# Sixteen one-column copies leave GpSimd for VectorE or ScalarE in a fused attention and FFT-mixing kernel

## The chip, the cores and the metric

The kernel runs on one core of one Trainium2 chip. The metric is the device time of one execution in microseconds (us), as a median over several executions. A profile takes one execution; its "span" was 1.8 us shorter than that execution's device time, so profiles and times can be set against each other. A run over 1.5% above the fastest of its kernel would be set aside as slow.

## The reference, cut to what matters

```
attn = softmax(normalise(q) @ normalise(k).T / tau) @ v     # 8 batches, 12 heads, 448 tokens, 64 wide
x    = heads of attn side by side                            # (8, 448, 768)
u    = x + real(fft(fft(x, axis=1), axis=2))
out  = u + relu(layernorm(u) @ w_ch1) @ w_ch2                # 768 -> 3072 -> 768
```

The two FFTs are matrix products with cosine and sine tables. The kernel halves them by folding: it adds and subtracts mirrored rows (giving F) and mirrored columns (giving G). Columns 0 and 192 of the fold are their own mirror images, so they are not added to anything; they are copied. That is one copy of a 128x8 tile per such column, two per batch, 16 in all.

## The kernel before

The program has its own list scheduler: each operation is planned with an estimated length and put at the end of one engine's queue, and each engine then runs its queue strictly in that order, waiting on semaphores (in the trace of this kernel VectorE's 893 instructions, ScalarE's 677 and TensorE's 5625 weight loads start in the line order of the built program). An operation planned for two engines goes to whichever the plan finds free first.

```python
        if dj < 2:                                     # in fold(): the self-mirrored column of block dj
            c = 192 * dj
            P.add("pool", lambda g: g.tensor_copy(G[:, :, :, c:c + 1], F[:, :, :, c:c + 1]), 0.25, pj, f"gc{dj}_{b}",
                  reads=[f"F0{dj}", f"F1{dj}"], writes=[f"Gc{dj}"])
        # ... cut: VectorE makes the rest of G (L834)
        # row FFT of this block, 8 matmuls (L847); it waits for G and for the copy
        P.add("pe", fn, 8 * t_mm(NK), pj, f"fs{blk}_{b}", reads=[f"Gc{blk}", f"G{blk}0", f"G{blk}1", "CSs"], ...)
```

GpSimd also issues the weight loads, twelve pieces of W1 and twelve of W2, at most three in flight: each issue waits until the load three places earlier has landed.

```python
            # in weights(): prev[-3] is the load three places earlier
            prev.append(P.add("pool", fn, 0.8, 9, nm, writes=[nm], dma=(nm, 16), after=[prev[-3]], serve=2.1))
```

Up to the first FFN matmul, the program fills planned pauses of TensorE with small matmuls ("fillers", L1097) whose results nobody reads. They are there to keep the engine busy: in the first profile, where they stop at 45.77 us and the engine stands, its granted clock falls to 0.50 from 48.7 to 58.9 us.

```python
                for _ in range(n):
                    r = pe.matmul(self.PS[:, bank, 450:512], self.ID[:], self.ID[:, 0:62], start=True, stop=True)
```

Of the kernel before, what the change touches and what calls it, by code (L numbers as in the profile page):

```python
# [290 lines left out]
def t_act(n, ptr=0):  # L291
    return 0.12 + 0.00089 * n + 0.093 * ptr


def t_dve(n, mode=1):
    return 0.1 + n / (960.0 * mode)
# [6 lines left out]
def t_mm(n):  # L303
    return max(0.036, n / 2400.0 + 0.0025)


def gp(ap, dims, off=0):

    return bass.AP(ap.tensor, ap.offset + off, [list(ap.ap[0])] + [list(d) for d in dims])


class Kern:
# [491 lines left out]
    def fold(self, b, dj, pj):  # L804

        P = self.P
        X = self.X[:].rearrange("p a (s c) -> p a s c", s=2)[:, :, :, 128 * dj:128 * dj + 128]
        AC, F, G = self.AC, self.F, self.G
        xr = [f"X{dj}", f"X{dj + 3}"]
        for i, o in ((0, AluOp.add), (2, AluOp.subtract)):  # L810
            P.add("dve", lambda v, i=i, o=o: v.tensor_tensor(AC[:, i:i + 2], X[:, 0:2], X[:, 2:4], o),
                  t_dve(512, 2), pj, f"fa{dj}_{b}", reads=xr, writes=[f"AC{i}"])
        for eo, o in ((0, AluOp.add), (1, AluOp.subtract)):
            op = P.add("dve", lambda v, eo=eo, o=o: v.tensor_tensor(F[:, eo, :, 128 * dj:128 * dj + 128], AC[:, :, 0, :], AC[:, :, 1, :], o),
                       t_dve(512, 2), pj, f"f{eo}{dj}_{b}", reads=["AC0", "AC2"],
                       writes=[f"F{eo}{dj}"] + ([f"UN{x}" for x in range(4)] if dj == 0 and eo == 0 else []),
                       after=[self.first_f] if dj or eo else [])
            if dj == 0 and eo == 0:
                self.first_f = op
        if dj < 2:  # L820

            c = 192 * dj
            P.add("pool", lambda g: g.tensor_copy(G[:, :, :, c:c + 1], F[:, :, :, c:c + 1]), 0.25, pj, f"gc{dj}_{b}",
                  reads=[f"F0{dj}", f"F1{dj}"], writes=[f"Gc{dj}"])
        if dj == 0:
            return

        blk = 2 - dj if dj == 2 else 1
        c0, n, m = ((1, 127, 128), (128, 64, 65))[blk]
        for i, o in ((0, AluOp.add), (1, AluOp.subtract)):  # L830
            def fn(v, i=i, o=o):
                f0, fs_ = (0, 2304) if i == 0 else (768, 768)
                g0, gs = (0, 6 * NG) if i == 0 else (2 * NG, 2 * NG)
                return v.tensor_tensor(gp(G[:], [[gs, 2], [NG, 2], [1, n]], g0 + c0), gp(F[:], [[fs_, 2], [384, 2], [1, n]], f0 + c0),  # L834
                                       gp(F[:], [[fs_, 2], [384, 2], [-1, n]], f0 + 384 - c0), o)
            P.add("dve", fn, t_dve(4 * n), pj, f"g{blk}_{b}", reads=[f"F{x}{y}" for x in range(2) for y in ((0, 2), (1, 2))[blk]],
                  writes=[f"G{blk}{i}"])
        tile = Tile("G")

        def fn(pe):  # L840
            bk = self.bank(tile)
            for eo in range(2):
                for s in range(2):
                    o = self.PS[0:m, bk + eo, s * NK:(s + 1) * NK]
                    for t in range(2):
                        k = 128 if t == 0 else RB
                        r = pe.matmul(o, G[0:k, eo, 2 * s + t, blk * 128:blk * 128 + m],  # L847
                                      self.CSs[0:k, t, s, :], start=(t == 0), stop=(t == 1))
            return r
        P.add("pe", fn, 8 * t_mm(NK), pj, f"fs{blk}_{b}", reads=[f"Gc{blk}", f"G{blk}0", f"G{blk}1", "CSs"], tiles=(tile,), acquire=tile, margin=0.2)  # L850
        for es, ah in ([(("act",), (0,)), (("dve",), (1,))] if b == 0 and blk else [(("act", "dve"), (0, 1))]):
            def ev(e, ah=ah):
                bk, a = self.bank(tile), slice(ah[0], ah[-1] + 1)
                o = self.Tt[0:m, 0:4 * SQ2].rearrange("p (a d k) -> p d a k", a=2, d=2)[:, blk, a]
                i = self.PS[0:m, bk + ah[0]:bk + ah[-1] + 1, 0:SQ2]
                if e is self.nc.scalar:
                    return e.activation(o, i, ACTF.Copy)  # L857
                return e.tensor_copy(o, i)
            n_ = len(ah) * SQ2
            P.add(es, ev, [t_act(n_) if e == "act" else t_dve(n_) for e in es], pj, f"te{blk}_{b}",  # L860
                  writes=[f"Tt{blk}" + ("b" if len(ah) == 1 and ah[0] else "")], after=[tile.users[0]], tiles=(tile,))
# [294 lines left out]
```

## Time and profile before

| | value |
|---|---|
| time, median of 3 | 625.41 us (624.96 to 626.06) |
| the profiled execution | 627.76 us, span 625.9 us |
| TensorE busy | 594.1 us, 95% of the span |
| VectorE, ScalarE, GpSimd busy | 63%, 55%, 16% |
| mean granted TensorE clock of the profiled execution | 0.986 |

Read it from the engine that is nearly always busy, and look for what its pauses wait for. The prediction below shows the lines.

### The profile page before, as it was taken

How to read it: one execution, taken by the hardware profiler on the slowest of the kernel's cores; microseconds unless marked ns; L12 is line 12 of the kernel's file. 1: busy time of each engine (PE TensorE's matmuls, PEld its weight loads, DVE VectorE, ACT ScalarE, POOL GpSimd, SP SyncE). 2: the span in 40 equal slices, each digit the busy share in tenths (PEclk: the TensorE clock that was granted, in tenths of full speed). 3: DMA queues.
4: the chain of work that ended last, by engine and by line, in shares of the span. 5: the costliest groups of instructions: out<-in, count | busy, mean ns of one | idle time of the engine just before them, and what ended most of it. 6: DMA issues, size and time to landing. Idle time of an engine off the chain costs nothing.

```text
span 625.9 us, 13629 instructions
## 1 busy us (share of the span) xinstructions
PE 594.1 (95%) x5607; PEld 388.3 (62%) x5625; DVE 391.3 (63%) x893; ACT 342.7 (55%) x677; POOL 98.4 (16%) x141
## 2 busy tenths in 40 slices
PE   4784889999999999999999999999999999999998
PEld 4564767767777566665646666666556666654464
DVE  7972997698777868887796679678644460010011
ACT  7870689426885388658666846772765015104400
POOL 8722411201003100300300040003000010010010
PEclk9996899999999999999999999999999999999999
DMA  7999949939729924985956299429200130000001
GB/s 185 123 212 208 148 77 190 90 94 188 131 55 121 183 69 95 137 154 117 128 69 158 70 122 165 90 53 133 65 1 2 39 88 26 25 28 25 1 26 75
DMA packets 187630, 62.03 MB, mean 99 GB/s; under 512 B 166704, under 2 KB 185264, under 8 KB 187568
## 3 DMA queue, kind: packets, MB, share of 16 engines
q1 hardware_dynamic: 129648, 38.35, 33.0%
q0 software_dynamic: 57920, 22.81, 27.7%
q8 instruction: 44, 0.72, 0.5%
q14 instruction: 18, 0.15, 0.1%
HBM read 51.90 MB, written 11.01 MB: 101 GB/s over the span
## 4 chain that ended last, share of the span: by engine, by line
PE 85%; DMA 5%; POOL 4%; DVE 3%; ACT 2%; issue 1%; POOLq 0%; DVEq 0%
PE PS L1000 35%; PE PS L1022 33%; PE PS L751 5%; PE PS L782 5%; DMA W1b<-in_moe_w_ch_dram 5%; PE PS L847 2%; PE PS L779 2%; PE PS L882 2%; ACT E L733 1%; DVE U L903 1%; PE PS L763 1%; PE PS L764 1%; POOL VB L713 1%; POOL UNT L440 0%; DVE ST L930 0%
## 5 line engine op out<-in xcount | busy, mean ns | idle before, releaser
L1000 PE MATMUL PS<-UNT,W1b 128*128 128x256 bf16 (+3 forms) x1423 | 232.7, 317 | 2.9 <-issue 1.0
L1022 PE MATMUL PS<-W2b,hT 128*128 128x384 bf16 (+2 forms) x1343 | 228.9, 326 | 0.1
L1000 PEld LDWEIGHTS PS<-UNT,W1b 128*128 128x128 bf16 x1440 | 130.4, 99 | 86.5 <-issue 3.0
L1022 PEld LDWEIGHTS PS<-W2b,hT 128*128 128x128 bf16 x1344 | 129.2, 98 | 82.3 <-issue 2.0
L733 ACT ACTIVATE E<-PS 128x900 bf16<-128x900 f32 (+1 forms) x192 | 149.8, 826 | 32.1 <-PE PS L751 26.6
L1009 ACT ACTIVATE hT<-PS 128x512 bf16<-128x512 f32 (+3 forms) x166 | 79.6, 480 | 99.5 <-PE PS L1000 98.0
L1031 DVE TENSOR_TENSOR OUTB<-PS,U 128x384 f32<-128x384 f32 (+2 forms) x56 | 31.2, 557 | 117.6 <-PE PS L1022 116.8
L1052 POOL DMA_INDIRECT out_dram<-OUTB,IDX x20 | 21.4, 1071 | 252.7 <-DVE OUTB L1031 118.1
L668 DVE TENSOR_REDUCE SS<-QH 128x6 f32<-128x384 f32 x84 | 45.3, 540 | 11.5 <-ACT QH L666 11.3
L1010 DVE TENSOR_SCALAR hT<-PS 128x256 bf16<-128x256 f32 (+3 forms) x74 | 37.0, 501 | 23.1 <-PE PS L1000 21.8
L782 PE MATMUL PS<-VB,E 128*128 128x65 bf16 x1152 | 51.0, 193 | 0.0
L782 PEld LDWEIGHTS PS<-VB,E 128*128 128x128 bf16 x1152 | 47.7, 97 | 1.6
L666 ACT ACTIVATE QH<-STG 128x384 f32<-128x384 f32 x84 | 43.5, 518 | 6.4 <-DVE SS L668 3.3
L751 PE MATMUL PS<-QT,KT 64*128 64x225 bf16 x576 | 42.9, 261 | 2.1 <-ACT E L733 1.7
L779 PE MATMUL PS<-VZ,E 128*128 128x130 bf16 x192 | 42.2, 220 | 1.6 <-DMA VB<-in_v_dram 1.3
L903 DVE TENSOR_TENSOR U<-SQT,X 128x384 bf16<-128x384 f32 (+3 forms) x80 | 41.0, 552 | 0.8
L675 DVE TENSOR_TENSOR QH<-STG,RN 128x768 bf16<-128x768 f32 x42 | 39.8, 950 | 0.3
L857 ACT ACTIVATE Tt<-PS 128x900 bf16<-128x900 f32 (+2 forms) x14 | 12.5, 892 | 40.5 <-PE PS L847 40.5
L796 DVE TENSOR_TENSOR X<-PS,RD 128x512 bf16<-128x512 f32 x48 | 33.1, 691 | 1.5
L751 PEld LDWEIGHTS PS<-QT,KT 64*128 64x128 bf16 x576 | 21.2, 94 | 20.3 <-ACT E L733 7.5
L713 POOL DMA_DIRECT2D VB<-in_v_dram x24 | 25.3, 1061 | 41.9 <-PE PS L782 41.6
L934 ACT ACTIVATE RS<-MV,cst 128x1 f32<-128x1 f32 x28 | 8.2, 291 | 42.4 <-DVE MV L932 41.1
(116 smaller groups left out, 491.5 us busy)
## 6 DMA issues: line engine op xcount, KB each, us to landing
STG<-in_q_dram SPq DMA_DIRECT2D x18, 384.0 KB, 4.9
STG<-in_k_dram SPq DMA_DIRECT2D x18, 384.0 KB, 4.7
VB<-in_v_dram POOLq DMA_DIRECT2D x24, 192.0 KB, 5.9
W1b<-in_moe_w_ch_dram POOLq DMA_DIRECT2D x12, 384.0 KB, 8.8
W2b<-in_moe_w_ch_dram POOLq DMA_DIRECT2D x12, 384.0 KB, 6.9
out_dram<-OUTB SPq DMA_DIRECT2D x7, 384.0 KB, 2.9
hT<-in_k_dram SPq DMA_DIRECT2D x2, 576.0 KB, 5.4
hT<-in_q_dram SPq DMA_DIRECT2D x2, 576.0 KB, 6.8
```

Of the source, the lines that this page charges most:

```text
L666: P.add("act", lambda a, sq=sq, src=buf[:, w * x:w * x + w]: a.activation(sq, src, ACTF.Square), t_act(w), pr, f"sq{i}_{b}", reads=bn, wri ...
L668: P.add("dve", lambda v, o=SS[:, i, H // ns * x:H // ns * (x + 1)], sq=sq: v.tensor_reduce(o, sq.rearrange("p (h d) -> p h d", d=DH), AX.X ...
L675: P.add("dve", lambda v, i=i, buf=buf, qh=qh: v.tensor_tensor(v3(qh), v3(buf), RN[:, i, :].unsqueeze(2).to_broadcast((128, H, DH)), AluOp. ...
L733: return a.activation(o, self.PS[:, bk:bk + nc_, 0:SQ2], ACTF.Exp, scale=1.0 / self.tau)
L751: i = pe.matmul(self.PS[:, bk + h, c0:c0 + NK], self.KT[r, jj, kt * 128:(kt + 1) * 128], self.QT[r, jj, cols], start=True, stop=True)
L779: pe.matmul(o, st(6), self.VZ[:, j, :], start=True, stop=False, skip_group_check=True)
L782: r = pe.matmul(o[:, 65 * h:65 * h + 65], st(2 * kt + h), self.VB[:, kt, 2 * j + h, :], start=False, stop=(h == 1 and kt == 2), skip_group ...
L903: return v.tensor_tensor(U[o0:o0 + n, ut, cs].rearrange("p (i e) -> p i e", e=2), src, X[i0:i0 + n, x, cs].rearrange("p (i e) -> p i e", e ...
L1000: r = pe.matmul(self.PS[:, bk, 0:n], self.W1b[:, j, ft * 128:(ft + 1) * 128], unT[:, j, cs], start=(j == 0), stop=(j == NJ - 1))
L1009: return e.activation(self.hT[:, ft, cs], self.PS[:, bk, 0:n], ACTF.Relu)
L1010: return e.tensor_relu(self.hT[:, ft, cs], self.PS[:, bk, 0:n])
L1022: r = pe.matmul(self.PS[:, bk, 0:n], self.hT[:, ft, 128 * i:128 * i + 128], self.W2b[:, ft, c0:c0 + n], start=(ft == 0), stop=(ft == NF - 1))
```

## The change

The intent is to take small copies off a queue that DMA issues block (in the first profile nine W1 issues stood 20.1 us in all for the landing of a load before them). The helper `copy` lets the plan choose ScalarE or VectorE.

```diff
-            P.add("pool", lambda g: g.tensor_copy(G[:, :, :, c:c + 1], F[:, :, :, c:c + 1]), 0.25, pj, f"gc{dj}_{b}",
-                  reads=[f"F0{dj}", f"F1{dj}"], writes=[f"Gc{dj}"])
+            self.copy(G[:, :, :, c:c + 1], F[:, :, :, c:c + 1], 8, 1, pj, f"gc{dj}_{b}", reads=[f"F0{dj}", f"F1{dj}"],
+                      writes=[f"Gc{dj}"])
```

Since a scheduler decides the order, the change also moves other instructions.

## The prediction

> **What bounds the kernel now.** I began with the page: the busy shares, then the 40 slices (each 15.6 us).
>
> ```profile
> PE 594.1 (95%) x5607; PEld 388.3 (62%) x5625; DVE 391.3 (63%) x893; ACT 342.7 (55%) x677; POOL 98.4 (16%) x141
> ...
> PE   4784889999999999999999999999999999999998
> ...
> PEclk9996899999999999999999999999999999999999
> ```
>
> TensorE is full from the seventh slice on; its holes lie in the first six, and the lowest digit after the start-up is the fourth slice (47 to 63 us), where the granted clock is also lowest. From the view by stretches, PE is busy 26.0 of 26.0 us from 100 to 126, and from 126 to 486 it is idle for only 1.8 us (0.39 + 0 + 0.27 + 0.17 + 0 + 0.96 over six stretches); 486 to 560 is all busy. So after about 100 us the time is the sum of TensorE's work, and only a hole near the start, or one newly made later, can change it. Which hole does the touched line own? The waits, longest in total first:
>
> ```profile
> POOL G L823 <- DVE F L814: 151.1, 7, 42.9
> ...
> PEld PS L847 <- POOL G L823: 9.5, 1, 9.5
> PE PS L847 <- POOL G L823: 9.4, 1, 9.4
> ```
>
> The columns are total us, times, longest. The 151.1 us are GpSimd waiting for work and cost nothing. The row to read is the last: in all eight batches TensorE waits for this copy once, for 9.4 us. The chain that ended last says where (start, duration, what):
>
> ```profile
> 39.90 13.89 DMA W1b<-in_moe_w_ch_dram
> ...
> 54.07 0.82 POOL W1b L470
> 54.89 0.23 POOL G L823
> ...
> 55.17 1.72 PE PS L847 x8
> ...
> 59.16 0.50 ACT SNQ L888
> ...
> 65.76 5.52 PE PS L1000 x60
> ```
>
> and the timeline around it tells what the copy itself had been waiting for:
>
> ```profile
> 44.20 0.76 DVE L814 TENSOR_TENSOR F<-AC 128x512 bf16<-128x512 bf16 x2
> 45.00 0.51 DVE L834 TENSOR_TENSOR G<-F 128x256 bf16<-128x256 bf16 x2
> ...
> 54.07 0.82 POOL L470 DMA_DIRECT2D W1b<-in_moe_w_ch_dram  x1 [4.41 <-DMA W1b<-in_moe_w_ch_dram]
> 54.89 0.23 POOL L823 COPY G<-F 128x8 bf16<-128x8 bf16 x1
> ```
>
> The copy's input F is complete at 44.20 + 0.76 = 44.96 and the rest of its G block at 45.51. The copy takes 0.23 us, yet starts at 54.89, because GpSimd's program has three W1 load issues in front of it (45.58, 48.84, 54.07), each waiting until the load three places earlier has landed.[...]
>
> [...] the copy, ready at 44.96, runs 9.9 us later, behind the issues. [...] the 16 copies take 218/232/572 ns (min/median/max), so speed of the copy is not the point, place in the queue is. [...] the nearest form in the trace (128x1, no pointer bias) takes 202 ns. [...] the clock is 0.50 from 48.7 to 58.9, the end of the hole and 3.7 us beyond it, and again 0.50 from 65.7 to 69.1.
>
> **The change part by part.** I compared the built programs' instruction orders.
>
> *Removed:* 16 copies (4.6 us) from GpSimd, which has 84% of its span free: worth nothing in itself. *Added:* 8 copies each on VectorE and ScalarE, 0.2 us each by the rows above (16 x 0.2 = 3.2 us, two engines with about 37% and 45% of the span free): beside other work except in batch 0. There the first copy lands on ScalarE among the exponentials of the last head pairs, where ScalarE runs without a gap from 31.8 to 39.6, so its 0.2 us is on the path. The second comes after the table loads (over at 42.54 + 1.28 = 43.82), so runs at once at 44.96.
>
> *Moved, the start:* the second row-FFT matmul group (L847) then waits for the later of G at 45.51, the copy at about 45.2, and the 14 filler matmuls before it in TensorE's order (45.20 + 0.57 = 45.77). I take 45.7 plus the 0.2 above = 45.9 in place of 55.17: 9.3 us earlier. From there to the first ScalarE copy (L888) took 59.16 - 55.17 = 3.99 us, mostly at half clock. The same steps warm: the batch's first such group, at full clock, needed 0.99 us from start to evacuation (41.42 to 42.41) against 1.76 (55.17 to 56.93), 0.77 less; the 8 column-FFT matmuls took 1.22 us here and half of 1.36 later, 0.54 less. So L888 starts at 45.9 + 3.99 - 1.3 = 48.6: 10.6 us earlier. The 6.6 us from L888 to the first FFN matmul (65.76) are vector and scalar work[...], so the FFN begins near 55.2. Its first 60 matmuls took 5.52 us with the half clock; at the later 0.84 us per 12 they would take 4.2. Whether the low stretch at 65.7 comes again depends on the short idle before it (62.82 to 64.55), which stays; I count one third of the 1.3 us: 0.4.
>
> *Is everything else there 10.6 to 12 us earlier?* Landing times from the trace's semaphore records: batch 1's q and k by 61.7, the first at 42.6 and first needed by ScalarE at about 63.7 - 10.6 = 53; the last three W1 chunks at 57.9, 61.2 and 63.3, needed from about 65 on (the last two FFN columns ran at 77.6); batch 1's last v piece at 79.24, first used at 91.43 - 10.6 = 80.8. All hold, the last by 1.6 us. The W2 pieces reuse batch 1's staging, so they follow the compute.
>
> *Moved, the middle:* TensorE's order is the same for the first half. From about batch 4 the program's own scheduler weaves attention among FFN matmuls differently: after the last column FFT 96 second-layer matmuls of that batch are left instead of 174. The counts of real work are equal, and that region has 1.8 us of idle to win or to double: I book -0.2 for added waits, plus or minus 1.
>
> Sum: 625.4 - 10.6 - 0.4 + 0.2 = 614.6 us, 1.7% less.
>
> **Rivals.** *A transfer takes the wait's place.* For: the windows view gives a DMA share above 1[...] through the hole and up to 78 us; the last v piece has only 1.6 us to spare. Against: the landing times above do not depend on TensorE. If v slips by 2 us, the time is about 616 to 617. *The new order makes holes.* For: the second half is reshuffled, and copies now sit in in-order queues of ScalarE and VectorE, where one waiting for F holds up exponentials and evacuations behind it. Against: each copy needs F that VectorE makes in the same breath, attention moves later relative to FFN, which lends it slack. If it happens, 2 to 5 us come back: 617 to 620. *The gain is absorbed*, since ScalarE and VectorE pace batch 1 (17.7 and 18.2 of 20 us busy from 80 to 100). For: PE idles 1.9 us there in their favour. Against: both were nearly idle in the hole (ScalarE 2.8, VectorE 4.0 of 14.2 us), so nothing was caught up there that must now be done elsewhere; their work moves with the start. Otherwise about 621. *It gains more:* full clock throughout the first FFN (0.9 more) and a tighter middle (1): 612.7.
>
> **Range and chances.** The start is well fixed at 10.6; clock and middle give about 1 us each way, holes weigh to the slow side: 612.6 to 617.5 holds it 8 in 10. 2% is 12.5 us, that is, under 612.9: it needs the clock and the middle both in favour, 0.11. Within 2%: 0.87. Slower by 2% would take a new stall larger than the one removed plus 12 us: 0.02.
>
> **What would show it.** In the changed profile, no wait of L847 above 1 us; its second group of batch 0 at 45 to 46.5 us; the fourth slice of PE and PEclk higher; the first L1000 at 54 to 56.5 us; PE idle from 126 us on still under 3 us. I would be wrong if L847 comes early but the first FFN does not (ScalarE's queue is blocked by a load or copy), if PE waits on VB, VZ, W1b or W2b between 56 and 115 us, or if idle stretches of over 0.5 us appear among the attention matmuls of the later batches.

10.6 (9.3 for the start of L847 and 1.3 for the steps at full clock), 0.4 and 0.2 are read from the first profile or are estimates from it. That a half clock goes with TensorE's standing still was my reading of two places in that profile; the table of profiles below comes back to it. I took the 6.6 us from L888 to the FFN to be the same at any clock of TensorE; they came out at 6.59 in the changed kernel. ScalarE's 65x450 eviction (L857) took 0.54 us and VectorE's (L858) 0.62 us at the clock of 0.50 in this profile, and the same at full clock in the changed kernel's profile. The DMA share named under "Rivals" was 1.27 to 1.35 from 44 to 55 us and 0.94 to 2.31 in the stretches from there to 78 us.

## The result, and the profile after

The changed kernel takes 617.89 us (median of 4, 616.94 to 618.09) against 625.18 us for the kernel before in the same rounds. Ratios here are the mean time of one kernel's fast runs over that of the other's in the same rounds, so not quite the ratio of the medians quoted. This one is 0.9882, with a 95% interval of 0.9862 to 0.9902: 1.2% faster, which counts as the same at 2%. The predicted class was right, the predicted 614.6 was 3.3 us too low, and the measured time lies just outside the range, whose upper end was 617.5.

The page of the changed kernel, with the same lines as before: busy time, then TensorE's busy tenths and its granted clock in 40 slices, now of 15.4 us.

```profile
PE 591.1 (96%) x5604; PEld 384.7 (62%) x5621; DVE 389.0 (63%) x896; ACT 346.5 (56%) x690; POOL 96.3 (16%) x125
...
PE   4788999999999999999999999999999999999998
...
PEclk8899999999999999999999999999999999999999
```

The 4 in the fourth slice has become an 8, and the clock there is 9. In the list of waits no row of L847 for the copy is left. The timeline around the place (start, length, engine, line, operation, and in brackets the idle time before it) shows what stands there instead.

```profile
44.28 0.76 DVE L814 TENSOR_TENSOR F<-AC 128x512 bf16<-128x512 bf16 x2
44.80 0.82 POOL L470 DMA_DIRECT2D W1b<-in_moe_w_ch_dram  x1 [5.24 <-DMA W1b<-in_moe_w_ch_dram]
45.08 0.24 ACT L1061 ACTIVATE G<-F 128x8 bf16<-128x8 bf16 x1 [1.04 <-DVE F L814]
45.08 0.51 DVE L834 TENSOR_TENSOR G<-F 128x256 bf16<-128x256 bf16 x2
...
46.51 0.46 PE L1097 MATMUL PS<-ID 128*128 128x62 bf16 x10 [2.04 <-issue]
...
46.81 0.96 PE L847 MATMUL PS<-CSs,G 128*65 128x225 bf16 x8
...
55.96 6.17 PE L1000 MATMUL PS<-UNT,W1b 128*128 128x128 bf16 x84 [0.17 <-ACT UNT L958]
```

The copy now runs at 45.08, as soon as F is there, while GpSimd goes on issuing loads. But the matmuls do not follow at once: TensorE stands for 2.04 us in the middle of a run of fillers, with nothing that the profile shows to wait for ("issue"), until 46.51. The FFN then starts at 55.96, against 65.76 in the first profile of before: 9.8 us earlier.

There is a second difference later: the two orders of TensorE part at about 240 us of the new profile. The stretch from 240 to 300 us, before and then after (stretch, length, and for TensorE, its weight loads, VectorE, ScalarE and GpSimd the busy us and count; granted clock; DMA share; GB/s):

```profile
240.00:300.00 60.00, 59.73 (x579) 38.30 (x581) 49.73 (x119) 43.24 (x87) 7.49 (x11) 1.00 0.82 124
```

```profile
240.00:300.00 60.00, 58.85 (x496) 35.75 (x500) 45.94 (x106) 35.68 (x76) 7.53 (x8) 1.00 0.70 109
```

TensorE's idle time there is 60 - 59.73 = 0.27 us before and 1.15 us after. Other stretches win some of that back: summed from 126 us to the end of the interleaved part (486 us before, 476 us after) the idle time is 1.8 us before and 2.4 us after, and no pause there is over 0.4 us. This small loss goes with the new interleaving.

So two profiles differ by 625.9 - 616.0 = 9.9 us of span, close to what the prediction subtracted, while the timed runs differ by 7.3 us. The experiments had to settle both: what carries the gain, and where 2 to 3 us of it went.

### The profile page after: what moved, and what is told of

Same layout as the page of the kernel before. It is cut to its first block, busy times and chain, and to the rows that moved or that the text cites. A ratio compares the mean times of both kernels' runs of the same rounds, so it can differ in the third digit from the quotient of the medians.

```text
span 616.0 us, 13590 instructions
## 1 busy us (share of the span) xinstructions
PE 591.1 (96%) x5604; PEld 384.7 (62%) x5621; DVE 389.0 (63%) x896; ACT 346.5 (56%) x690; POOL 96.3 (16%) x125
## 4 chain that ended last, share of the span: by engine, by line
PE 87%; DVE 6%; ACT 2%; POOL 2%; issue 2%; DMA 1%; POOLq 0%; DVEq 0%; ACTq 0%
PE PS L1000 34%; PE PS L1022 34%; PE PS L782 5%; PE PS L751 5%; PE PS L779 2%; PE PS L847 2%; PE PS L882 2%; ACT E L733 2%; DVE U L903 1%; DMA VB<-in_v_dram 1%; DVE ST L930 1%; PE PS L763 1%; PE PS L764 1%; PE PS L1097 1%; DVE OUTB L1031 0%
## 5 line engine op out<-in xcount | busy, mean ns | idle before, releaser
L1000 PE MATMUL PS<-UNT,W1b 128*128 128x256 bf16 (+3 forms) x1424 | 230.6, 315 | 3.4 <-issue 1.3
L1000 PEld LDWEIGHTS PS<-UNT,W1b 128*128 128x128 bf16 x1440 | 129.2, 98 | 87.2 <-ACT hT L1009 3.0
L1009 ACT ACTIVATE hT<-PS 128x384 bf16<-128x384 f32 (+3 forms) x170 | 81.0, 477 | 94.7 <-PE PS L1000 93.2
L1010 DVE TENSOR_SCALAR hT<-PS 128x256 bf16<-128x256 f32 (+3 forms) x70 | 35.3, 505 | 27.6 <-PE PS L1000 26.4
L794 DVE RECIPROCAL RD<-PS 128x8 f32<-128x8 f32 x48 | 9.9, 206 | 32.2 <-PE PS L782 32.0
L857 ACT ACTIVATE Tt<-PS 128x900 bf16<-128x900 f32 (+2 forms) x15 | 13.4, 893 | 28.1 <-PE PS L847 28.1
```

The costliest lines, as they stand in the source:

```text
L1000: r = pe.matmul(self.PS[:, bk, 0:n], self.W1b[:, j, ft * 128:(ft + 1) * 128], unT[:, j, cs], start=(j == 0), stop=(j == NJ - 1))
L1009: return e.activation(self.hT[:, ft, cs], self.PS[:, bk, 0:n], ACTF.Relu)
L1010: return e.tensor_relu(self.hT[:, ft, cs], self.PS[:, bk, 0:n])
```

## The experiments

Twelve runs were made, in three calls of four; within a call all ran on the same chip, and each call had another one. All gave correct results.

The theory: the one copy that stands behind weight-load issues in batch 0 carries the whole change, and the error of the prediction lies in its reference point and in the pause. The rivals: the other 15 copies, the new order, or GpSimd's own speed matter.

**The kernel before again.** No edit.

> The kernel before, unchanged, with its own profile. Question: was the first profile of it (span 625.9, that execution 627.76 us) typical of its timed runs (median 625.18)? Theory A (the profiled run was an unlucky one: its hole of 9.4 us and its half-clock stretches were longer than usual): this run times at 624.0 to 626.1 and its profile, span near 623.4, shows the wait of L847 for the copy at 6.5 to 8 us, or no half-clock stretch at 65.7 us. Rival B (the hole is always 9.4 us and the changed kernel lost 3 us elsewhere): span and hole as in the first profile, 9 to 10 us.

Measured: 625.72 us (ratio 0.9988), span 624.6. The profile has the wait at 7.8 us, after a pause of 2.12 us among the fillers, so that L847 starts at 54.92, about where it did before (55.17). The first FFN matmul comes at 65.59, and the half clock that followed it in the first profile is missing. So theory A holds half: this execution, at 626.45 us, was faster than the first for the clock, not for the hole. (The wait for the copy is counted from the last filler, so the longer pause among the fillers, 2.12 us against 0.96, takes off most of the difference between 9.4 and 7.8.) More looks follow below.

**Only one copy moved.** After scheduling, the second copy of batch 0 is taken out of GpSimd's queue and put on VectorE behind its F; every other queue keeps its order.

```diff
         self.est = self.P.schedule()
+        self.move(["gc1_0"], "dve")      # out of order["pool"], into order["dve"] right behind the F it reads
```

> Only the second copy of batch 0 goes to VectorE, right behind the F that it reads; the other 15 stay on GpSimd and every other queue keeps the order of the kernel before. Theory: this one copy carries the whole change: 617 to 618.5 us, as the changed kernel (617.9). Rival (the new order in the middle, or the other 15 copies, cost or give something): clearly different from 617.9, e.g. 615.5 to 616.5 if the new order cost 1.5 to 2 us.

Measured: 616.56 us, ratio 0.9838 (0.9817 to 0.9859). One copy out of sixteen carries the whole gain, and a little more than the changed kernel has: this is 1.3 us below its 617.89, though in another call. The time lies below the 617 to 618.5 of the theory and next to the 615.5 to 616.5 of the rival, so it left open what the new order costs.

**The copy stays on GpSimd, ahead of the loads.**

```diff
+        q = self.P.order["pool"]
+        op = next(o for o in q if o.name == "gc1_0")
+        q.remove(op)
+        q.insert(next(i for i, o in enumerate(q) if o.name == "gc0_0") + 1, op)
```

> All copies stay on GpSimd; only the second copy of batch 0 is placed ahead of the last three W1 load issues in GpSimd's own order. Theory (place in the queue, not the engine): the wait of L847 for it vanishes and the time is that of one_moved within 1 us, 617 to 618.5. Rival (GpSimd itself is the trouble, slow or held up by VectorE): the wait stays at 2 us or more, or the loads behind the copy come late, 620 to 625.

Measured: 618.66 us, ratio 0.9872 (0.9848 to 0.9895). Its timeline:

```profile
44.47 0.76 DVE L814 TENSOR_TENSOR F<-AC 128x512 bf16<-128x512 bf16 x2
...
45.29 0.35 POOL L823 COPY G<-F 128x8 bf16<-128x8 bf16 x1 [3.75 <-DVE F L814]
46.18 0.84 POOL L470 DMA_DIRECT2D W1b<-in_moe_w_ch_dram  x1 [0.54 <-POOL G L823]
46.36 0.83 PE L1101 MATMUL PS<-ID 128*128 128x62 bf16 x14 [1.85 <-issue]
47.00 1.32 PE L847 MATMUL PS<-CSs,G 128*65 128x225 bf16 x6
```

GpSimd does the copy right when F is ready, and L847 starts at 47.00, as with one_moved (46.91). The engine is not the point; the place in the queue is. The time missed both limits that I had set, 618.5 and 1 us from one_moved: it is 2.1 us slower. Its profile was in half clock from 46.5 to 49.9 and, across the first FFN matmuls, from 56.7 to 60.1; the FFN started at 57.18 in place of 56.07 and the rest took 1.1 us longer. That accounts for the difference of the two profiled executions (619.14 and 616.96). Whether the other three runs, at 617.27 to 619.51, had the same is not recorded stretch by stretch; two of them have mean clocks of 0.989 and 0.992.

**All sixteen on VectorE, all other orders kept.**

```diff
+        self.move([f"gc{d}_{b}" for b in range(self.nb) for d in (0, 1)], "dve")
```

> All 16 copies go to VectorE, each right behind its F, with every other queue in the order of the kernel before. Theory: the other 15 copies are off the path: within 0.7 us of one_moved. Rival (3 us of added VectorE work is on the path): 1 to 3 us slower than one_moved. Against the changed kernel (617.9) it shows what its new order in the middle costs or gives.

Measured: 617.19 us, ratio 0.9866 (0.9837 to 0.9895), median 0.63 us above one_moved, with one of four runs at 619.84. By the means the difference is 1.4 us, half of it from that one run. The other 15 copies add nothing that these runs resolve; a small cost is not excluded (the part after the FFN's start took 559.32 us against 559.05).

**The changed kernel beside one_moved, five rounds.** No new edits.

> The changed kernel as it is, beside one_moved2 on one chip. Theory (the new order of the middle gives back a little): 0.7 to 2 us slower than one_moved2, most of it between 126 us and the end of the attention, where its first profile has 2.4 us of TensorE idle against 1.8 before. Rival (the two are equal and the difference of the earlier calls was the chip or the clock): within 0.5 us of one_moved2.

> Again only the second copy of batch 0 moved, for the comparison with after_again: 616 to 617, some 9.5 us under before.

Measured: 617.44 us (ratio 0.9869, 0.9848 to 0.989) for the changed kernel and 617.68 us (0.985, 0.983 to 0.9869) for one_moved. The changed kernel was expected 0.7 to 2 us slower and was not, by the medians; one_moved2 missed its own 616 to 617. The medians are level and the intervals overlap, so the times leave open whether the new order costs anything. The profiles say more; see the table below.

**Wide fillers.** In every profile with small fillers looked at so far the pause before L847 came in front of the same matmul, the one with number 603 counted from 0, wherever that stood in the run of fillers (behind 66 of 80 before, behind 70 of 80 after), and there is no semaphore wait there. Other long pauses came at number 476 and number 730, 127 matmuls away. In the trace's packet records a transfer on the queue that the page lists as "instruction" starts 0.1 to 1.5 us before the pause begins, and the pause ends 2.3 to 2.5 us after that transfer's start in all six profiles checked: 42.74 to 45.20 us in the first of before, 44.16 to 46.51 in the changed kernel. The earlier the transfer, the shorter the pause (1.50 us ahead of a pause of 0.96 us, 0.31 ahead of one of 2.04). So the suspicion was that TensorE ran out of instructions: 62-column fillers use one pair of them every 31 ns (66 in 2.04 us). The edit does about the same length of filling with a sixth of the instructions.

```diff
-                for _ in range(n):
-                    r = pe.matmul(self.PS[:, bank, 450:512], self.ID[:], self.ID[:, 0:62], start=True, stop=True)
+                for j in range(0, n, 6):
+                    k = min(n - j, 6)
+                    r = pe.matmul(self.PS[:, bank, 0:85 * k], self.ID[:], gp(self.ID[:, 0:85], [[0, k], [1, 85]]), start=True, stop=True)
```

> one_moved with the filler matmuls made wide: one instruction of up to 510 columns in place of six of 62, for the same length. In all profiles so far TensorE pauses in front of its matmul number 603, in the middle of a run of fillers with no semaphore wait in it, for 1 to 2.3 us, and a transfer on the instruction queue starts as it pauses; other pauses come 127 matmuls before or behind. Theory (TensorE waits for its own instructions, which small fillers use up fast): the pause of 2 us at 44 to 46.5 us goes, the second L847 group starts at 45.6 to 46 in place of 46.8 to 47.1, and the time falls by about 1 us, to 615 to 616. Rival (the pause is a wait for VectorE or ScalarE that shows as issue): the group still starts at 46.8 or later and the time stays.

Measured: 616.11 us, ratio 0.984 (0.9825 to 0.9856), against 617.68 and 0.985 for one_moved2 in the same rounds. The timeline:

```profile
41.80 2.85 PE L1111 MATMUL PS<-ID 128*128 128x510 bf16 x13
...
44.36 0.35 DVE L823 COPY G<-F 128x8 bf16<-128x8 bf16 x1
44.45 0.50 DVE L834 TENSOR_TENSOR G<-F 128x256 bf16<-128x256 bf16 x2
45.00 0.73 PEld L847 LDWEIGHTS PS<-CSs,G 128*65 128x65 bf16 x8 [0.71 <-DVE G L834]
45.00 0.98 PE L847 MATMUL PS<-CSs,G 128*65 128x225 bf16 x8 [0.36 <-DVE G L834]
```

The pause is gone: TensorE fills until 44.65 and then waits only for G itself. From the first L847 group to the second it is 4.22 us here (40.78 to 45.00) against 5.44 to 5.53 in the two profiles of one_moved. This profile's first FFN matmul is at 54.18, the earliest of all. In time the gain is about 1 us by the means (616.11 against 617.08), within the spread of the runs. The group came earlier than the 45.6 to 46 expected and the median 0.1 us above the 615 to 616. The pause goes when the fillers have fewer instructions, and the rival, a wait for VectorE or ScalarE, would have kept it. That TensorE stood for its instructions is my reading of the transfers and the counts, not a thing shown: the edit also changes which matmuls have the numbers 476, 603 and 730, and where the transfers on that queue fall (41 in place of 44), and no run separates a slower use of instructions from that.

> The kernel before with the wide fillers alone. Theory: the pause lay inside the hole that the copy makes, so nothing is won there: L847 still starts at 54.5 to 55.5 and the time is within 1 us of before. Rival (the fillers are worth something elsewhere at the start): 1 us or more faster.

Measured: 625.48 us, ratio 0.9992 (0.9975 to 1.0009), L847 at 53.42. As expected the pause cost the kernel before nothing, because it lay inside the hole. (The start is 1.1 us earlier than the lower end that I gave; the load landed earlier in this execution, which is the subject of the next runs.)

**Two more looks at the kernel before.** No edit, one profile each.

> The kernel before, one more profile. Theory (the time of one execution follows the start of the first FFN matmul, which hangs on the landing of W1 loads, plus 1.2 us if the half clock falls into the first FFN): time = start of the first L1000 + 560.8 +- 0.5 us, or + 562 with half clock behind that start; the start anywhere between 63.5 and 66. Rival (executions differ somewhere else): the sum misses by over 1 us.

> As before_look1, a second look: the same sum, and with the other profiles of this kernel a spread of the hole of 1 us or more.

Measured: 625.08 and 626.02 us; the sums give 64.00 + 560.8 = 624.8 and, with half clock behind the start, 63.99 + 562 = 626.0. Both hold. The end of the hole in the first of them:

```profile
52.11 0.82 POOL L470 DMA_DIRECT2D W1b<-in_moe_w_ch_dram  x1 [3.13 <-DMA W1b<-in_moe_w_ch_dram]
52.92 0.23 POOL L823 COPY G<-F 128x8 bf16<-128x8 bf16 x1
53.21 1.32 PEld L847 LDWEIGHTS PS<-CSs,G 128*65 128x65 bf16 x8 [6.21 <-POOL G L823]
53.21 1.72 PE L847 MATMUL PS<-CSs,G 128*65 128x225 bf16 x8 [6.09 <-POOL G L823]
...
64.00 1.21 PE L1000 MATMUL PS<-UNT,W1b 128*128 128x128 bf16 x15 [0.17 <-ACT UNT L958]
```

The same issue that came at 54.07 in the first profile comes at 52.11, because the load it waits for landed 2 us earlier. In four profiles of the unchanged kernel the wait for the copy is 9.4, 7.8, 6.1 and 5.4 us. Part of that spread is the pause among the fillers, since the wait is counted from the last of them (0.96 us in the first profile, 2.12 to 2.25 in the other three). What moves the time is when the copy is let through: L847 starts at 55.17, 54.92, 53.21 and 53.35. The hole ends when the weight loads of that execution let it.

**The copy behind two of the three issues.** The edit of pool_ahead with `+ 3` in place of `+ 1`.

> As pool_ahead, with the copy put behind two of the three W1 load issues (the third follows it). Theory (the hole is as long as the issues in front of the copy wait): the copy runs when the second issue is done, at 48.5 to 50.5 us, the second L847 group follows at once, and about 4.5 to 5.5 us of the gain are left: 620 to 622 us. Rival (the hole has another cause that the moves remove by chance, or loads behind the copy get late): at 617 to 618.5 as pool_ahead, or at 624 and more.

Measured: 621.7 us, ratio 0.9933 (0.9904 to 0.9961). Its timeline:

```profile
48.19 0.82 POOL L470 DMA_DIRECT2D W1b<-in_moe_w_ch_dram  x1 [3.03 <-DMA W1b<-in_moe_w_ch_dram]
49.00 0.23 POOL L823 COPY G<-F 128x8 bf16<-128x8 bf16 x1
49.28 1.32 PEld L847 LDWEIGHTS PS<-CSs,G 128*65 128x65 bf16 x8 [4.29 <-POOL G L823]
49.28 1.72 PE L847 MATMUL PS<-CSs,G 128*65 128x225 bf16 x8 [4.17 <-POOL G L823]
```

With one issue fewer in front, part of the gain appears; with none, all of it. The hole follows the place of the copy among the issues, as the theory says.

> The changed kernel with the wide fillers. Theory: the pause of 2 us goes here too, 1 us off: 616 to 617; and if the new order of the middle costs 0.5 to 1 us, it stays above one_wide (616.1, ratio 0.984) by that, at a ratio of 0.985 to 0.986. Rival (order of the middle costs nothing): ratio 0.984 or below.

Measured: 616.66 us, ratio 0.985 (0.9826 to 0.9874); in its profile L847 starts 4.15 us behind the first group, so the pause is gone here too. The time is within the expected 616 to 617 and the ratio at the lower end of the theory's 0.985 to 0.986; the interval covers the rival's 0.984 as well.

**All profiles in one table.** Times in us; "idle before L950" is how long TensorE stood before the six transposes just ahead of the FFN; "rest" is the span minus the start of the first FFN matmul (L1000); the last column says whether half clock fell on the first FFN matmuls.

| profile | execution | second L847 group | idle before L950 | first L1000 | rest | half clock there |
|---|---|---|---|---|---|---|
| before, first | 627.76 | 55.17 | 1.74 | 65.76 | 560.16 | yes |
| before_again | 626.45 | 54.92 | 1.25 | 65.59 | 559.06 | no |
| before_look1 | 625.08 | 53.21 | 0.92 | 64.00 | 559.25 | no |
| before_look2 | 626.02 | 53.35 | 1.74 | 63.99 | 560.19 | yes |
| before_wide | 624.89 | 53.42 | 0.89 | 63.91 | 559.17 | no |
| one_moved | 616.96 | 46.91 | 0.38 | 56.07 | 559.05 | no |
| one_moved2 | 617.86 | 47.38 | 0.38 | 56.53 | 559.49 | no |
| one_wide | 615.32 | 45.00 | 0.90 | 54.18 | 559.34 | no |
| all_moved | 617.33 | 47.05 | 0.38 | 56.21 | 559.32 | no |
| pool_ahead | 619.14 | 47.00 | 1.73 | 57.18 | 560.12 | yes |
| pool_mid | 621.7 | 49.28 | 1.73 | 59.70 | 560.16 | yes |
| changed kernel, first | 617.8 | 46.81 | 0.26 | 55.96 | 560.03 | no |
| after_again | 616.79 | 45.95 | 0.45 | 55.28 | 559.70 | no |
| after_wide | 617.43 | 46.05 | 0.89 | 55.22 | 560.40 | no |

Each execution's time is its FFN start, plus the rest, plus 1.8; that holds by definition, and shows only where executions differ. With the old order the rest is 559.05 to 559.49 without the half clock and 560.12 to 560.19 with it: that clock costs about 0.9 us when it falls there. With the new order it is 559.70 to 560.40 without any half clock there. All three values lie above all seven of the old order; the means are 560.04 and 559.24, so the new interleaving costs about 0.8 us in these profiles, which the timed runs are too scattered to confirm.

The half clock falls on the FFN in exactly the four profiles in which TensorE had stood 1.73 or 1.74 us before L950; in the other ten it had stood 1.25 us or less. Before, and then in the changed kernel:

```profile
64.55 0.51 PE L950 MATMUL PS<-ID,F 128*128 128x128 bf16 x6 [1.74 <-DVE F L939]
```

```profile
53.38 1.11 PE L1097 MATMUL PS<-ID 128*128 128x62 bf16 x33 [1.29 <-issue]
54.75 0.51 PE L950 MATMUL PS<-ID,F 128*128 128x128 bf16 x6 [0.26 <-DVE F L939]
```

In the changed kernel the next pause among the fillers, at matmul number 730, holds 33 of them back until 53.38, so that they end just before L950 and little idle time is left there. That the half clock follows the longer stand is so in all 14 profiles, but no run of its own tests it, and it is no rule for every pause: those of 2.05 and 2.29 us at number 603 in the changed kernel and in one_moved drew no half clock.

## Why the prediction was wrong in its number and right in its main mechanism

**What bounds the kernel, and the place of the hole: right.** A single copy behind load issues in batch 0 held TensorE; one_moved, pool_mid and pool_ahead show it from three sides.

**The copies themselves: right.** The 8-element copy on ScalarE took 0.24 us where I had 0.2 (the eight there took 224 to 239 ns). The other 15 do not show (all_moved).

**The start: mechanism right, size off by 0.76 us.** I put L847 at 45.9 and the FFN at 55.2; they came at 46.81 (0.3 us outside the 45 to 46.5 that it named as a sign) and 55.96. The 9.3 us from one to the other were 9.15. What was missing is the pause among the fillers, which I read as TensorE waiting for instructions (not shown). The same pause was in front of me in the first profile, 0.96 us at 44.25, harmless inside the hole; I read the fillers as ending at 45.77 whatever happened.

**The FFN's clock and the middle: right in sum, by luck.** The prediction took 560.16 of rest in the first profile to 560.16 - 0.4 + 0.2 = 559.96; the changed kernel's was 560.03. Two errors cancel. The 0.4 was a third of an estimated 1.3, because the idle stretch before the FFN "stays"; it did not stay, it shrank from 1.74 to 0.26 us, and the half clock went altogether, worth about 0.9. The new order cost about 0.8 rather than 0.2 (which the text books as "-0.2" and the sum rightly adds). Nor do the two stretches at half clock that the prediction names show one length of idle time that brings it: the one from 48.7 us began 2.9 us into the hole, and the one from 65.7 us came after a stand of only 1.74 us.

**The step that failed is the sum: "625.4 - 10.6 - 0.4 + 0.2".** All terms had been read from one profiled execution of 627.76 us, and I subtracted them from the median of other executions, 625.41. From the execution that they belong to, the sum gives 627.76 - 10.8 = 616.96; the changed kernel's profiled execution took 617.8, 0.84 more, nearly all of it the pause. The error splits without remainder worth naming: 2.35 us for the wrong base (627.76 - 625.41), 0.76 for the pause, 0.1 for the rest and 0.1 for the changed kernel's median over its profiled execution, together 3.3.

**"The start is well fixed at 10.6" was wrong for the same reason.** The hole depends on when weight loads land: the FFN of the unchanged kernel began between 63.99 and 65.76 in four executions. The changed kernel takes the landings off the path, so it does not gain a fixed amount; it gains more where the hole was longer. The first profile showed the longest hole of the four and the half clock besides. Against the timed runs the gain was 7.3 us in the first rounds and 8.5 us in the second (means 617.77 against 626.26).

**The rivals.** No transfer took the wait's place: neither W1b, W2b nor batch 1's v pieces held TensorE between 56 and 115 us. Nothing was absorbed on the way, since the rest is the same length from wherever the FFN starts. Holes in the new order came, but for about 0.8 us, none of them over 0.4 us, not 2 to 5.

Of the two kernels and the variants, one_wide is the fastest by its ratio: 0.984, with an interval of 0.9825 to 0.9856, against 0.9869 (0.9848 to 0.989) for the changed kernel in the same rounds. The intervals touch. What stays open is whether the 0.8 us of the new order shows in time, and why the pause among the fillers goes.

## What to carry to other kernels

An instruction that costs 0.2 us can hold the busiest engine for as long as whatever stands in front of it in its queue waits (here a copy of 0.23 us held it for 5.4 to 9.4 us); so look at what a small operation is queued behind before asking which engine does it faster. When a term is read from one profile, subtract it from the time of that execution, and find out how much that term varies from one execution to the next before calling it fixed. A pause that hides inside a larger wait comes out when the larger wait goes (here 2.04 us in front of matmul number 603).
